# Attention with a gated block on one core: keys loaded in transposable order, weight sums stored in thirds, the key scale in the exponential, three raw weight chunks

## The chip, the cores and the metric

The kernel runs on one core of one Trainium2 chip. The metric is the device time of one execution in microseconds (us); lower is better.

## The reference, cut to what matters

```python
S, D, Hq, Dh, Sk, W, F = 2048, 640, 32, 192, 2048, 512, 1536      # all tensors bf16
xn = layernorm(x)                                                 # 2048 x 640, no gain or bias
q = (xn @ wq).reshape(S, 32, 192)                                 # wq: 640 x 6144
k, v = k_cache[:, Sk-W:], v_cache[:, Sk-W:]                       # last 512 positions of each head
p = softmax(einsum("qhd,hkd->hqk", q, k) * 192 ** -0.5)           # no mask
s = einsum("hqk,hkd->qhd", p, v).reshape(S, 6144) @ wo            # wo: 6144 x 640
h = sigmoid(xn @ w_gate) * (xn @ w_up)                            # gated block
out = x + s * silu(h @ w_down)
```

## The kernel before, in words

Two parts follow each other. The **gated block** works on four blocks of 512 rows (`s` = 0 to 3). For each of 12 slices `f` of the hidden width, PE multiplies by gate and up weights (L433), ACT takes the sigmoid (L438), and DVE multiplies both into `hT_sb` (L439). Then PE multiplies by `wd_sb` in four tiles of 128 rows (L485, 12 slices each, every one of which needs the whole of `hT_sb[:, f]`); ACT and DVE form the silu (L492, L493), and POOL stores the tile to DRAM (L499).

The **attention** works on pairs of heads, two pairs to a group, eight groups. A run is a group with one half of the rows (1024), so there are 16 runs, two for each group. Each run has 16 score groups (L625: six matmuls with the transposed keys `kT` into two PSUM banks, then the exponential on ACT, L629, from there into `E`), and then eight value products (L639), whose result DVE divides by the row sum (L645, L646) into `o_st`; SP transposes `o_st` by DMA (L652), and the product with `wo` of the run before (L682) is put between the value products. The queries of the next run are made between the score groups. `q_after` is the list written by hand that says which query slot follows which score group.

The queries are not made by a plain product. Rows and weights are cut in halves, and seven products of sums take the place of eight (`query_slots`): the weights stand in four forms for each group, `w0`, `TA`, `TB` and `TC`, each `[128, 5, 384]` in f16, of which partitions 0 to 63 and 64 to 127 hold different operands. Each matmul on them uses 64 partitions, and two run beside each other. The third `u` of a head's 192 columns is taken out of the weights with a step of three (`T[rr, c, u::PC]`, L576).

To get the weights into f16, the first part of the program finds the largest weight (`scan_load`, `scan_fold`, `set_scale`, `set_scale2`). All weights are multiplied by a power of two, `w_up` (L226), and the keys by its inverse, `w_down` (L150), so that the scores are right again. The weights of a group come in five chunks of 128 rows. For each chunk:

- `load_raw` (L211): two DMAs issued by POOL into one of two buffers `raw`.
- `scale_w` (L224): ACT scales the whole chunk in place (L226) and copies two parts into `w0` (L227, L228).
- `sum_w` (L230): DVE forms the sums `TB`, `TA`, `TC` (L233, L234, L236, L237), ACT copies one part (L235).

A buffer is loaded again only when the sums of the chunk before in it are done. `load_raw` stands in POOL's queue, so POOL waits there, and all that POOL issues afterwards waits too. For group 0 this goes on in the fourth block (`s` = 3), beside the sigmoids: `scale_w` after slices 0, 2, 5, 7, 10, `sum_w` after slices 1, 3, 6, 8, 11. For group 1 it is in run 0. For the later groups it is among the value products of the runs with the first half of the rows, by the lists `sum_at` and `scale_at`.

The keys of a pair of heads: `load_kn` (L138) loads one head as it lies in DRAM into one buffer `kn_sb` (POOL's queue); `sort_k` (L145) multiplies it on POOL by `w_down` and writes it into `k_sb` (one buffer) with the columns sorted by their remainder by three, in the order that the transpose takes; `turn_k` (L156) transposes `k_sb` by DMA on SP into one of two `kT`. Pair 0 of group g + 1 is turned at the start of the value products of the second run of group g, pair 1 after the fourth of these value products.

PSUM has eight banks; `bank2` gives them in pairs, 0 and 1 being pair 0. Score groups use banks 4 and 5 or 6 and 7 in turn. Everything else takes a pair from a ring, or from `bank_order` where this isn't empty. The first queries (run 0) have nothing to hide under; their results leave PSUM by ACT (`on_act`), and ACT's queue has the load of `wo_g` (L530) ahead of them.

Of the kernel before, what the change touches and what calls it, by code (L numbers as in the profile page):

```python
# [17 lines left out]
def kernel(  # L18
# [71 lines left out]
    ident = const.tile([P, P], BF16, name="ident")  # L90
    make_identity(nc, ident[:])

    eps_t = const.tile([P, 1], F32, name="eps_t")
    nc.vector.memset(eps_t[:], eps)

# [15 lines left out]
    raw_pool = qctx.enter_context(tc.tile_pool(name="raw_pool", bufs=2, **rs))  # L111
# [8 lines left out]
    mx = const.tile([P, 1], F32, name="mx")  # L120
    w_up = const.tile([P, 1], F32, name="w_up")
    w_down = const.tile([P, 1], F32, name="w_down")
# [13 lines left out]
    kn_of, k_of = {}, {}  # L136

    def load_kn(key, i=0):  # L138
        hk = (2 * (key[0] * G + key[1]) + i) // rep
        kn_of[key] = k_pool.tile([P, KC, DH], BF16, name="kn_sb")  # L140
        nc.gpsimd.dma_start(
            kn_of[key][:], A_k_cache[0, hk, Sk - W:Sk, :].rearrange("(p k) d -> p k d", k=KC),
        )

    def sort_k(key):  # L145
        k_sb = k_pool.tile([P, KC, PC, 2, HF], BF16, name="k_sb")
        for i in range(2):
            if i > 0:
                load_kn(key, i)
            nc.gpsimd.tensor_scalar(  # L150
                k_sb[:, :, :, i, :], kn_of[key][:].rearrange("p k (e j) -> p k j e", j=PC),
                w_down[:, 0:1], None, op0=ALU.mult,
            )
        k_of[key] = k_sb

    def turn_k(key):  # L156
        kT = kt_pool.tile([P, KC * PC, P], BF16, name="kT")
        nc.sync.dma_start_transpose(kT[:], k_of[key][:].rearrange("p k j i e -> p (k j i e)"))
        kT_t[key] = kT
# [37 lines left out]
    def set_scale(wm, mx_row):  # L197
        nc.vector.tensor_reduce(
            mx[:], wm[:].rearrange("p c n -> p (c n)"), axis=mybir.AxisListType.X, op=ALU.max)
        nc.gpsimd.dma_start(mx_d[:].rearrange("o p -> p o"), mx[:])  # L200
        nc.gpsimd.dma_start(mx_row[:], mx_d[:].to_broadcast([P, P]))

    def set_scale2(mx_row):
        nc.vector.tensor_reduce(mx[:], mx_row[:], axis=mybir.AxisListType.X, op=ALU.max)
        nc.vector.tensor_scalar(mx[:], mx[:], 1e-30, None, op0=ALU.max)
        bits = mx[:].bitcast(I32)
        nc.vector.tensor_single_scalar(bits, bits, 0x7F800000, op=ALU.bitwise_and)
        nc.vector.tensor_scalar(w_down[:], mx[:], 1.0 / 4096, None, op0=ALU.mult)
        nc.vector.reciprocal(w_up[:], w_down[:])
# [10 lines left out]
    def b(g, c, r, k, j):  # L220
        n = GC // 2
        return raw_t[g, c][r, k, j * n:(j + 1) * n].bitcast(F16)

    def scale_w(g, c):  # L224
        raw, w0 = raw_t[g, c][:], w_t[g][0]
        nc.scalar.activation(raw.bitcast(F16), raw, AF.Copy, scale=w_up[:, 0:1])  # L226
        nc.scalar.activation(w0[LO, c], b(g, c, LO, 0, 0), AF.Copy)  # L227
        nc.scalar.activation(w0[HI, c], b(g, c, HI, 1, 0), AF.Copy)  # L228

    def sum_w(g, c):  # L230
        _, TA, TB, TC = w_t[g]
        a, tt = slice(0, P), nc.vector.tensor_tensor
        tt(TB[:, c], b(g, c, a, 1, 1), b(g, c, a, 0, 1), ALU.subtract)  # L233
        tt(TA[:, c], TB[:, c], b(g, c, a, 0, 0), ALU.add)  # L234
        nc.scalar.activation(TB[HI, c], b(g, c, HI, 1, 1), AF.Copy)  # L235
        tt(TC[:, c], b(g, c, a, 1, 0), TA[:, c], ALU.subtract)  # L236
        tt(TA[HI, c], b(g, c, HI, 0, 1), b(g, c, HI, 0, 0), ALU.subtract)  # L237


    with ExitStack() as bctx:  # L240
# [7 lines left out]
        xt_pool = bctx.enter_context(tc.tile_pool(name="xt_pool", bufs=1))  # L248

# [171 lines left out]
        for s in range(NST):  # L421
# [4 lines left out]
            for f in range(NF):  # L426
# [30 lines left out]
                elif s == 2 and f < 4:  # L457
# [5 lines left out]
                elif s == 3:  # L463
# [36 lines left out]
            if s == 0:  # L500
                for hp in range(G):
                    load_v(0, hp, nc.gpsimd)
                for pp in range(1):
                    load_kn((0, pp))
# [9 lines left out]
    small = ctx.enter_context(tc.tile_pool(name="small", bufs=4))  # L514
# [32 lines left out]
    def query_slots(r, on_act, gamma):  # L547
# [27 lines left out]
        def wt(T, u):  # L575
            return lambda rr, c: T[rr, c, u::PC]  # L576
# [25 lines left out]
        def s4_split(u, bx, b):  # L602
# [4 lines left out]
        gx, gw, gy = gamma  # L607
        return [
            lambda: s1(0, 0, 1), lambda: s1(1, 2, 3),
            lambda: s2(0, 0, 1), lambda: s2(1, 2, 3),  # L610
            lambda: s3(0, 0, 1, False), lambda: s3(1, 2, 3, True),
            lambda: s4_pair(0, 0, 1, 1),
# [4 lines left out]
    def stage_s(r, i, pp, c, k):  # L617
# [11 lines left out]
        nc.scalar.activation(E_t[r, i, pp][:, c, :, :], ps, AF.Exp, scale=scale_qk)  # L629
# [92 lines left out]
    slots = query_slots(0, True, (4, 5, 6))  # L722
    for n, k in enumerate((0, 1, 7, 2, 3, 8, 4, 5, 9, 6, 10)):
# [112 lines left out]
```

## Time and profile before

| what | value |
|---|---|
| median of 3 runs | 952.66 us (951.15 to 952.68) |
| the profiled execution: time | 952.68 us |
| the profiled execution: span, first to last instruction | 950.9 us |
| mean granted clock of TensorE | 0.986 |
| DMA: packets, bytes | 186612, 100.37 MB |

How to read the lines: PE is TensorE's matmuls, PEld its weight loads, DVE VectorE, ACT ScalarE, POOL GpSimd, SP SyncE. A `q` behind an engine's name (SPq) is its queue, which issues DMAs. L226 is line 226 of the kernel. A group of instructions reads: line, engine, operation, written<-read by the names of the program, shapes, count | busy time in us, mean of one in ns | idle time of the engine just before them and what ended it. A line of the timeline reads: start in us, length in us, engine, line, operation, count, and in brackets the idle time before it with who ended that. A line of the waits reads: who waited <- for whom: us in total, times, the longest. A stretch reads: its two ends and length in us, then for each of PE, PEld, DVE, ACT, POOL that has instructions there the busy time and the count, then the granted clock, the share of the DMA engines, GB/s.

### The profile page before, as it was taken

What the parts mean: (1) busy time and instruction counts of PE and PEld (TensorE: products, weight loads), DVE (VectorE), ACT (ScalarE), POOL (GpSimd) and SP (SyncE); (2) the same over time, 40 slices, a digit from 0 to 9 for tenths busy, and PEclk for the clock granted to TensorE, in tenths of its full rate; (3) what the DMA queues carried; (4) which work ended last, traced back from release to release, by engine and by line L of the source; (5) the groups of instructions that cost most, each with busy time, mean ns of one, the idle gap of its engine ahead of it and who ended that gap; (6) DMA issues with size and microseconds to landing.
All of it is one profiled execution on the core that took longest, in us unless ns stands there. A gap on an engine that the chain in (4) does not pass through costs nothing. (4 is left out here: it accounts for less than half of the span.)

```text
span 950.9 us, 18447 instructions
## 1 busy us (share of the span) xinstructions
PE 904.0 (95%) x7706; PEld 552.2 (58%) x7785; DVE 652.6 (69%) x1090; ACT 446.0 (47%) x527; POOL 209.0 (22%) x216
## 2 busy tenths in 40 slices
PE   8999995689899999999999999999999999999987
PEld 5545442346475757575747575666566666666554
DVE  5879854357666776687668667866786678666556
ACT  4333362378425661566076607561755276423330
POOL 0042034110220132013202310321033002203951
PEclk9999999799899999999999999999999999999999
DMA  9875255222442456156415460635084416156724
GB/s 305 240 230 134 36 129 92 63 72 42 93 97 55 83 126 107 45 101 125 110 25 121 107 134 1 153 82 125 2 180 70 109 30 147 42 101 167 177 49 117
DMA packets 186612, 100.37 MB, mean 106 GB/s; under 512 B 153312, under 2 KB 178912, under 8 KB 186528
## 3 DMA queue, kind: packets, MB, share of 16 engines
q1 hardware_dynamic: 156848, 56.87, 28.8%
q0 software_dynamic: 9408, 29.93, 12.0%
q10 hardware_dynamic: 20272, 12.39, 5.0%
q8 instruction: 61, 1.00, 0.4%
q14 instruction: 23, 0.19, 0.1%
HBM read 57.87 MB, written 5.24 MB: 66 GB/s over the span
## 5 line engine op out<-in xcount | busy, mean ns | idle before, releaser
L629 ACT ACTIVATE E<-ps_all 128x1024 bf16<-128x1024 f32 x256 | 253.3, 1022 | 300.9 <-DMA v_sb<-in_A_v_cache_dram 165.2
L682 PE MATMUL ps_all<-wo_g,oT 128*128 128x128 bf16 (+2 forms) x1474 | 225.1, 296 | 6.4 <-DVE o_sb L697 3.1
L625 PE MATMUL ps_all<-qT,kT 64*128 64x512 bf16 x1536 | 199.4, 381 | 4.7 <-DVE o_st L646 3.0
L639 PE MATMUL ps_all<-v_sb,E 128*128 128x193 bf16 x2048 | 189.5, 247 | 2.4 <-DVE o_sb L697 1.8
L639 PEld LDWEIGHTS <-E 128*128 128x128 bf16 x2048 | 168.7, 98 | 20.9 <-issue 9.2
L682 PEld LDWEIGHTS <-oT 128*128 128x128 bf16 x1536 | 121.5, 98 | 82.5 <-issue 6.4
L573 DVE TENSOR_TENSOR qT<-ps_all,qp 128x512 bf16<-128x512 f32 x176 | 116.8, 688 | 53.0 <-PE ps_all L539 40.5
L560 DVE COPY qp<-ps_all 128x512 f32<-128x512 f32 x150 | 100.7, 688 | 61.5 <-PE ps_all L539 61.5
L214 POOL DMA_DIRECT2D raw<-in_A_wq_dram x80 | 47.9, 604 | 406.9 <-ACT wB L235 299.5
L625 PEld LDWEIGHTS <-kT 64*128 64x128 bf16 x1536 | 82.0, 95 | 89.6 <-issue 14.1
L646 DVE TENSOR_TENSOR o_st<-ps_all,rden 128x768 bf16<-128x768 f32 x128 | 122.5, 957 | 6.1 <-DMA oT<-o_st 1.7
L150 POOL TENSOR_SCALAR k_sb<-kn_sb,w_down 128x768 bf16<-128x768 bf16 x32 | 71.7, 2240 | 135.8 <-DMA kT<-k_sb 85.8
L226 ACT ACTIVATE raw<-raw,w_up 128x1536 f16<-128x1536 bf16 x40 | 63.0, 1575 | 43.0 <-DMA raw<-in_A_wq_dram 42.2
L485 PE MATMUL ps_all<-wd_sb,hT_sb 128*128 128x128 bf16 (+1 forms) x377 | 56.4, 310 | 15.7 <-DVE hT_sb L439 11.1
L439 DVE TENSOR_TENSOR hT_sb<-ps_all,sig_sb 128x512 bf16<-128x512 f32 x48 | 32.6, 684 | 41.0 <-ACT sig_sb L438 30.2
L539 PE MATMUL ps_all<-X,w 64*128 64x512 bf16 x420 | 52.7, 378 | 4.7 <-DVE o_st L646 2.9
L485 PEld LDWEIGHTS <-hT_sb 128*128 128x128 bf16 x384 | 30.9, 101 | 41.3 <-DVE hT_sb L439 11.7
L716 DVE TENSOR_TENSOR acc<-ps_all,acc 128x640 f32<-128x640 f32 x48 | 39.6, 825 | 21.9 <-PE ps_all L682 21.9
L539 PE MATMUL ps_all<-XA,wA 64*128 64x512 f16 x420 | 52.9, 376 | 1.3 <-ACT qp L558 0.9
L645 DVE RECIPROCAL rden<-ps_all 128x4 f32<-128x4 f32 x128 | 23.2, 181 | 44.5 <-PE ps_all L639 43.4
L539 PE MATMUL ps_all<-XB,wB 64*128 64x512 f16 x420 | 53.1, 376 | 0.4 <-ACT qp L558 0.2
L438 ACT ACTIVATE sig_sb<-ps_all 128x512 bf16<-128x512 f32 x48 | 28.1, 597 | 40.1 <-PE ps_all L433 37.1
(115 smaller groups left out, 766.8 us busy)
## 6 DMA issues: line engine op xcount, KB each, us to landing
raw<-in_A_wq_dram POOLq DMA_DIRECT2D x80, 192.0 KB, 4.2
wo_g<-in_A_wo_dram ACTq DMA_DIRECT2D x7, 960.0 KB, 5.2
kn_sb<-in_A_k_cache_dram POOLq DMA_DIRECT2D x32, 192.0 KB, 2.8
v_sb<-in_A_v_cache_dram ACTq DMA_DIRECT2D x28, 192.0 KB, 3.1
gB_d<-gB_sb POOLq DMA_DIRECT2D x16, 160.0 KB, 2.8
gBa_sb<-gB_d SPq DMA_DIRECT2D x16, 160.0 KB, 3.9
xa_sb<-in_A_x_dram SPq DMA_DIRECT2D x16, 160.0 KB, 3.8
out_dram<-o_sb SPq DMA_DIRECT2D x15, 160.0 KB, 1.8
```

The source lines that it names most:

```text
L150: nc.gpsimd.tensor_scalar(k_sb[:, :, :, i, :], kn_of[key][:].rearrange("p k (e j) -> p k j e", j=PC), w_down[:, 0:1], None, op0=ALU.mult,)
L214: eng.dma_start(raw[r], wq_r[:, c, :, g * GC:(g + 1) * GC])
L226: nc.scalar.activation(raw.bitcast(F16), raw, AF.Copy, scale=w_up[:, 0:1])
L485: nc.tensor.matmul(oB_ps[:, d0:d0 + dsz], lhsT=hT_sb[:, f, q * P:(q + 1) * P], rhs=wd_sb[:, f, d0:d0 + dsz], start=(f == 0), stop=(f == NF ...
L539: nc.tensor.matmul(ps_all[:, b, :], lhsT=w(r, c), rhs=x[r, c, :], start=(first and k == 0), stop=(k == len(cs) - 1), skip_group_check=True,)
L560: nc.vector.tensor_copy(dst, part(b))
L573: nc.vector.tensor_tensor(q_out(i, u, pp), part(b), t[:], ALU.add)
L625: nc.tensor.matmul(ps[:, b, :], lhsT=kT[h, c * PC + j, :], rhs=qT_t[r][i, j][h, pp, :], start=(j == 0), stop=(j == PC - 1),)
L629: nc.scalar.activation(E_t[r, i, pp][:, c, :, :], ps, AF.Exp, scale=scale_qk)
L639: nc.tensor.matmul(o_ps[:, q // 2, q % 2, 0:DH + 1], lhsT=E[:, c, h, q * P:(q + 1) * P], rhs=vt[:, c, 0:DH + 1], start=(c == 0), stop=(c = ...
L646: nc.vector.tensor_tensor(o_st[:, :, h * DH:(h + 1) * DH].rearrange("p (b i) d -> p b i d", b=2), o_ps[:, :, :, 0:DH], rden[:].to_broadcas ...
L682: nc.tensor.matmul(oA[:, d0 - base:d0 - base + dsz], lhsT=oT_t[r, i, pp][:, q * PC + j, :], rhs=wo_t[runs[r][1]][:, cc, d0:d0 + dsz], star ...
```

## The change

- **Keys.** `load_kn` and `sort_k` are gone. `load_k` loads both heads of a pair by two DMAs of POOL's queue straight into `k_sb`, 64 columns of a head at a time beside 64 of the other, which is the layout that `turn_k` takes. The columns are cut into three consecutive thirds instead of by the remainder by three.
- **Scale.** The keys are no longer multiplied. `w_down` is multiplied once by 192 ** -0.5 and is the exponential's scale, read from memory.
- **Weights.** The sums and `w0` are written in thirds, so that a query product takes 128 consecutive columns.
- **Raw chunks.** Three buffers; the third chunk of group 0 is loaded in the third block, each load is put three chunks ahead, and the lists are moved accordingly.
- **Order.** The first queries take banks 2 to 7 and 0 instead of 0 to 6; runs 0 and 15 begin their value products with pair 2.
- **Small tiles.** `ident` and `eps_t` go into a pool of the gated block; `mx`, `w_up` and `w_down` share a tile; `rden` has two buffers instead of four.

```diff
-    raw_pool = qctx.enter_context(tc.tile_pool(name="raw_pool", bufs=2, **rs))
+    raw_pool = qctx.enter_context(tc.tile_pool(name="raw_pool", bufs=3, **rs))
...
-    def load_kn(key, i=0):
-        hk = (2 * (key[0] * G + key[1]) + i) // rep
-        kn_of[key] = k_pool.tile([P, KC, DH], BF16, name="kn_sb")
-        nc.gpsimd.dma_start(
-            kn_of[key][:], A_k_cache[0, hk, Sk - W:Sk, :].rearrange("(p k) d -> p k d", k=KC),
-        )
-
-    def sort_k(key):
-        k_sb = k_pool.tile([P, KC, PC, 2, HF], BF16, name="k_sb")
+    def load_k(key):
+        k_sb = k_pool.tile([P, KC * PC, 2, HF], BF16, name="k_sb")
         for i in range(2):
-            if i > 0:
-                load_kn(key, i)
-            nc.gpsimd.tensor_scalar(
-                k_sb[:, :, :, i, :], kn_of[key][:].rearrange("p k (e j) -> p k j e", j=PC),
-                w_down[:, 0:1], None, op0=ALU.mult,
+            hk = (2 * (key[0] * G + key[1]) + i) // rep
+            nc.gpsimd.dma_start(
+                k_sb[:, :, i, :],
+                A_k_cache[0, hk, Sk - W:Sk, :].rearrange("(p k) (j e) -> p (k j) e", k=KC, e=HF),
             )
         k_of[key] = k_sb
...
         nc.vector.reciprocal(w_up, w_down)
+        nc.vector.tensor_scalar(w_down, w_down, scale_qk, None, op0=ALU.mult)
...
-    def b(g, c, r, k, j):
+    def part_w(g, c, r, k, j):
         n = GC // 2
-        return raw_t[g, c][r, k, j * n:(j + 1) * n].bitcast(F16)
+        w = raw_t[g, c][r, k, j * n:(j + 1) * n].bitcast(F16)
+        return w.rearrange("p (h j e) -> p h j e", h=2, e=HF)
+
+    def sums_w(g, c, r, i):
+        return w_t[g][i][r, c].rearrange("p (j h e) -> p h j e", h=2, e=HF)
...
-        tt(TB[:, c], b(g, c, a, 1, 1), b(g, c, a, 0, 1), ALU.subtract)
-        tt(TA[:, c], TB[:, c], b(g, c, a, 0, 0), ALU.add)
+        TA, TB, TC = (sums_w(g, c, a, i) for i in range(1, 4))
+        tt(TB, part_w(g, c, a, 1, 1), part_w(g, c, a, 0, 1), ALU.subtract)
+        tt(TA, TB, part_w(g, c, a, 0, 0), ALU.add)
...
-                elif s == 2 and f < 4:
+                elif s == 2 and f < 5:
                     load_raw(0, f - 2, nc.gpsimd)
...
                         sum_w(0, c)
-                        load_raw((c + 2) // NCD, (c + 2) % NCD, nc.gpsimd)
-                    if f == 2:
-                        sort_k((0, 0))
-                        turn_k((0, 0))
-                        load_kn((0, 1))
-                    elif f == 5:
-                        sort_k((0, 1))
-                        turn_k((0, 1))
-                        load_kn((1, 0))
+                        load_raw((c + 3) // NCD, (c + 3) % NCD, nc.gpsimd)
+                    if f in (2, 6):
+                        turn_k((0, f // 4))
+                        load_k(divmod(f // 4 + 1, G))
...
-            return lambda rr, c: T[rr, c, u::PC]
+            return lambda rr, c: T[rr, c, u * P:(u + 1) * P]
...
-        nc.scalar.activation(E_t[r, i, pp][:, c, :, :], ps, AF.Exp, scale=scale_qk)
+        nc.scalar.activation(E_t[r, i, pp][:, c, :, :], ps, AF.Exp, scale=w_down)
...
-    slots = query_slots(0, True, (4, 5, 6))
+    slots = query_slots(0, True, (2, 3), (4, 5), (6, 7, 0))
...
-            load_raw(1, n // 5 + 2, nc.gpsimd)
-    sum_at = {2: (3,), 4: (4,)}, {0: (0,), 1: (1,), 3: (2,), 5: (3,), 6: (4,)}
-    scale_at = {0: (3,), 2: (4,)}, {1: (2,), 3: (3,), 5: (4,)}
+            load_raw(1, n // 5 + 3, nc.gpsimd)
+    sum_at = {2: (3,), 6: (4,)}, {0: (0,), 1: (1,), 3: (2,), 4: (3,), 6: (4,)}
+    scale_at = {0: (3,), 2: (4,)}, {0: (2,), 3: (3,), 4: (4,)}
...
-            bank_order[:] = []
+            bank_order[:] = [2, 3, 0, 1] * 2
         else:
-            bank_order[:] = [0, 1, 0, 1] + [2, 3, 0, 1] * 3 if r > 0 else []
+            bank_order[:] = [0, 1, 0, 1] + [2, 3, 0, 1] * 3 if r > 0 else [2, 3, 0, 1] * 2
...
         elif pi == 1 and g + 1 < NG:
-            sort_k((g + 1, 0))
             turn_k((g + 1, 0))
-            load_kn((g + 1, 1))
-            sort_k((g + 1, 1))
-            if g + 2 < NG:
-                load_kn((g + 2, 0))
+            load_k((g + 1, 1))
...
             if k == 3 and pi == 1 and g + 1 < NG:
                 turn_k((g + 1, 1))
+                if g + 2 < NG:
+                    load_k((g + 2, 0))
...
-            for c in range(2):
+            for c in range(3):
                 load_raw(g + 2, c, nc.gpsimd)
```

More of the change, by code (lines that the diff above doesn't have):

```diff
@@ L119 @@
     w_t = {}
-    mx = const.tile([P, 1], F32, name="mx")
-    w_up = const.tile([P, 1], F32, name="w_up")
-    w_down = const.tile([P, 1], F32, name="w_down")
+    w_sc = const.tile([P, 3], F32, name="w_sc")
+    mx, w_up, w_down = (w_sc[:, i:i + 1] for i in range(3))
     NV = 2 * G
@@ L218, in weight_tiles @@
         w_t[g] = [wq_pool.tile([P, NCD, GC // 2], F16, name=f"w{i}") for i in "0ABC"]
-    def b(g, c, r, k, j):
+    def part_w(g, c, r, k, j):
         n = GC // 2
-        return raw_t[g, c][r, k, j * n:(j + 1) * n].bitcast(F16)
+        w = raw_t[g, c][r, k, j * n:(j + 1) * n].bitcast(F16)
+        return w.rearrange("p (h j e) -> p h j e", h=2, e=HF)
+    def sums_w(g, c, r, i):
+        return w_t[g][i][r, c].rearrange("p (j h e) -> p h j e", h=2, e=HF)
     def scale_w(g, c):
[L225 to L228, printed above, removed]
+        raw = raw_t[g, c][:]
+        nc.scalar.activation(raw.bitcast(F16), raw, AF.Copy, scale=w_up)
+        for k, r in enumerate((LO, HI)):
+            nc.scalar.activation(sums_w(g, c, r, 0), part_w(g, c, r, k, 0), AF.Copy)
     def sum_w(g, c):
-        _, TA, TB, TC = w_t[g]
         a, tt = slice(0, P), nc.vector.tensor_tensor
[L233 to L237, printed above, removed]
+        TA, TB, TC = (sums_w(g, c, a, i) for i in range(1, 4))
+        tt(TB, part_w(g, c, a, 1, 1), part_w(g, c, a, 0, 1), ALU.subtract)
+        tt(TA, TB, part_w(g, c, a, 0, 0), ALU.add)
+        nc.scalar.activation(sums_w(g, c, HI, 2), part_w(g, c, HI, 1, 1), AF.Copy)
+        tt(TC, part_w(g, c, a, 1, 0), TA, ALU.subtract)
+        tt(sums_w(g, c, HI, 1), part_w(g, c, HI, 0, 1), part_w(g, c, HI, 0, 0), ALU.subtract)
     with ExitStack() as bctx:
@@ L248 @@
         xt_pool = bctx.enter_context(tc.tile_pool(name="xt_pool", bufs=1))
+        ident = bone.tile([P, P], BF16, name="ident")
+        make_identity(nc, ident[:])
+        eps_t = bone.tile([P, 1], F32, name="eps_t")
+        nc.vector.memset(eps_t[:], eps)
         x_even = X1
@@ L789 @@
                     sum_w(new_t, c)
-                    if c + 2 < NCD:
-                        load_raw(new_t, c + 2, nc.gpsimd)
+                    if r > 0 and c + 3 < NCD:
+                        load_raw(new_t, c + 3, nc.gpsimd)
                 for c in scale_at[r > 0].get(k, ()):
```

41 lines of the change are left out of this document (18 added, 23 removed).

## The prediction

> **What bounds the kernel now.** I read the page first, then the stretches of the span, and then the timeline where a stretch shows idle time on the matrix engine.
>
> ```profile
> span 950.9 us, 18447 instructions
> PE 904.0 (95%) x7706; PEld 552.2 (58%) x7785; DVE 652.6 (69%) x1090; ACT 446.0 (47%) x527; POOL 209.0 (22%) x216
> ```
>
> PE is busy for 904.0 of 950.9 us, so 46.9 us idle are all that reordering can win, besides time lost to a slower clock. The change takes no matmul away. The stretches (us, then busy time of each engine, granted clock, DMA) say where the idle time lies:
>
> ```profile
> 151.80:185.90 34.10, 17.09 (x94) 8.62 (x96) 13.69 (x19) 11.36 (x16) 10.96 (x13) 0.80 0.35 73
> 203.60:228.10 24.50, 24.00 (x201) 11.74 (x200) 15.11 (x25) 18.96 (x21) 1.19 (x2) 0.93 0.11 30
> 242.00:248.00 6.00, 5.99 (x30) 2.56 (x31) 2.00 (x4) 2.05 (x2) 2.38 (x3) 0.51 0.96 218
> 291.00:890.00 599.00, 592.59 (x5473) 379.09 (x5523) 428.81 (x718) 304.18 (x341) 118.25 (x117) 1.00 0.44 93
> ```
>
> From 291 to 890 us, which is most of the sixteen attention runs, PE idles 599.00 - 592.59 = 6.4 us: little to win there. But in the 34.1 us in which the fourth gate block multiplies by wd_sb, 17.0 us are idle, and the clock that is granted afterwards is low (0.80 on average). The timeline of that stretch (start, length, engine, line, and in brackets the idle time before it and who ended it):
>
> ```profile
> 143.54 17.17 SPq L158 DMA_TRANSPOSE kT<-k_sb  x2
> 144.41 1.23 POOL L214 DMA_DIRECT2D raw<-in_A_wq_dram  x2
> 144.95 0.60 ACT L438 ACTIVATE sig_sb<-ps_all 128x512 bf16<-128x512 f32 x1
> 151.78 2.19 POOL L150 TENSOR_SCALAR k_sb<-kn_sb,w_down 128x768 bf16<-128x768 bf16 x1 [6.14 <-DMA kT<-k_sb]
> 152.51 1.57 ACT L226 ACTIVATE raw<-raw,w_up 128x1536 f16<-128x1536 bf16 x1 [6.97 <-DMA raw<-in_A_wq_dram]
> 155.85 4.62 PE L485 MATMUL ps_all<-wd_sb,hT_sb 128*128 128x512 bf16 x19 [4.06 <-ACT sig_sb L438]
> 167.94 1.57 ACT L226 ACTIVATE raw<-raw,w_up 128x1536 f16<-128x1536 bf16 x1 [9.10 <-DMA raw<-in_A_wq_dram]
> 172.00 6.23 PE L485 MATMUL ps_all<-wd_sb,hT_sb 128*128 128x512 bf16 x29 [9.99 <-DVE hT_sb L439]
> ```
>
> Read it backwards. PE waits for hT_sb, which needs the sigmoid on ACT. ACT works in order and stands in front of a weight chunk (L226) whose load has not landed. The load is late because POOL, which issues it, first sorts keys (L150) and waits for a key transpose to free k_sb. So two raw buffers and a sort on the loading queue cost this stage two stops.
>
> **The change, part by part.** *A, the fourth gate block.* Chunk 2 is now loaded in the block before. Chunk 3 goes out after the first sum, as chunk 2 did. Chunk 4 goes out after the second sum, and what stands ahead of it on POOL is only the two loads of key pair 1, not a sort. Those loads wait for the transpose of pair 0, which SP can issue as soon as its four swap copies are out, since its keys were loaded two blocks earlier. Both L226 waits (6.97 and 9.10 us) should go. What is late next is ACT itself. Durations:
>
> ```profile
> L226 ACT ACTIVATE raw<-raw,w_up 128x1536 f16<-128x1536 bf16 x40 | 63.0, 1575 | 43.0 <-DMA raw<-in_A_wq_dram 42.2
> L227 ACT ACTIVATE w<-raw 64x384 f16<-64x384 f16 x35 | 18.3, 523 | 1.1
> L235 ACT ACTIVATE wB<-raw 64x384 f16<-64x384 f16 x35 | 18.0, 513 | 25.4 <-DVE wA L234 25.4
> L439 DVE TENSOR_TENSOR hT_sb<-ps_all,sig_sb 128x512 bf16<-128x512 f32 x48 | 32.6, 684 | 41.0 <-ACT sig_sb L438 30.2 <-PE ps_all L433 10.5
> L234 DVE TENSOR_TENSOR wA<-wB,raw 128x384 f16<-128x384 f16 x35 | 12.5, 358 | 1.2
> ```
>
> The sigmoid of step 7 ends at 144.95 + 0.60 = 145.55. Scaling a chunk is 1.575 + 2 x 0.523 = 2.62, to 148.2; sigmoid 8 to 148.8; its hT 0.68, two sums 0.72 and L235's 0.51 bring ACT to 150.7; sigmoids 9 and 10 to 151.9; chunk 4 to 154.5; sigmoid 11 and its hT to 155.8. The down product starts at 155.85 - 4.06 = 151.8. Its length without waits is that of the block before (L485 alone):
>
> ```profile
> 92.00:125.70 33.70, 12.91 (x94) 7.42 (x96) 1.00 0.43 82
> ```
>
> 12.9 us for 48 steps, 0.27 each, so PE asks for hT 11 at 151.8 + 11 x 0.27 = 154.8: a wait of 1.0, 1.2 with hand-overs. The block ends at 151.8 + 12.9 + 1.2 = 165.9.
>
> ```profile
> 185.92 3.42 PE L539 MATMUL ps_all<-X,w 64*128 64x512 bf16 x30 [1.65 <-DVE gB_sb L493]
> 188.38 0.45 ACTq L530 DMA_DIRECT2D wo_g<-in_A_wo_dram  x1
> 203.63 0.61 PE L625 MATMUL ps_all<-qT,kT 64*128 64x512 bf16 x2 [1.22 <-DVE qT L573]
> ```
>
> Now it ends at 185.92 - 1.65 = 184.27. Gain **18.4**. The raw loads go out earlier still, so nothing waits behind them.
>
> *B, the first queries.* With products in banks 2 to 7 the first need not wait 1.65 us for the last gate tile. I cost that at nothing all the same: ACT is held until 188.38 by the load of wo_g, and ACT empties the banks, so the wait returns three products later. At the end, the first scores no longer share banks with the last query product: of 1.22 us what is left after one score group, about 0.5, comes back at the second (banks 6 and 7). Gain 0.7. The clock of 0.93 over 24.5 us is 1.7 us, which goes if the idle time shrinks; sum **2.4** (between 0 and 3.5).
>
> *C, between runs 0 and 1.* Run 0 has no output products, so its value products run faster than DVE empties them:
>
> ```profile
> 237.27 0.96 DVE L646 TENSOR_TENSOR o_st<-ps_all,rden 128x768 bf16<-128x768 f32 x1 [0.95 <-DMA oT<-o_st]
> 239.92 0.96 DVE L646 TENSOR_TENSOR o_st<-ps_all,rden 128x768 bf16<-128x768 f32 x1
> 242.01 2.74 PE L625 MATMUL ps_all<-qT,kT 64*128 64x512 bf16 x12 [3.04 <-DVE o_st L646]
> 242.08 0.96 DVE L646 TENSOR_TENSOR o_st<-ps_all,rden 128x768 bf16<-128x768 f32 x1
> ```
>
> Scores need banks 4 to 7, which now hold the last two value products. In the new order they hold the fifth and sixth. The fifth is empty at 237.27 + 0.96 = 238.2, before PE is done (242.01 - 3.04 = 238.97). The last weight sum moves behind the seventh, so the sixth follows after 1.1 (two take 242.08 - 239.92 = 2.16), at 239.3, and the seventh at 240.4, or some 0.9 later if its o_st waits for a transpose again. A score group takes 2.74 / 4 = 0.68 at the full clock, so two end at 240.3 and the first query slot waits up to 1.0; the second waits for the eighth, behind that weight sum, about as long. I put 0.85 and 0.95, so 3.04 becomes 1.8 (between 0 and 3.0). The half clock (0.51 over 6 us, 2.9 us lost) should go, since no wait is long. Gain **4.1** (1 to 6).
>
> *D, the other runs.* Waits from 291 to 890 us:
>
> ```profile
> DVE wB L233 <- ACT raw L226: 9.4, 6, 2.7
> PE ps_all L539 <- DVE o_st L646: 2.9, 4, 1.1
> ```
>
> DVE stands before sums whose chunk is not scaled, then empties the last value product late, and PE waits. With chunk 2 loaded a run ahead, and three steps between the loads of 3 and 4 and their use, the 9.4 should go. Gain **2.5** (-2 to 5; the lower end if the sums cost more, below).
>
> *E, the last run.*
>
> ```profile
> 920.42 10.83 PE L639 MATMUL ps_all<-v_sb,E 128*128 128x193 bf16 x128 [1.84 <-DVE o_sb L697]
> ```
>
> Its value products start in banks 4 and 5 instead of the banks that the last output product holds. Gain **1.8**.
>
> *What costs nothing.* Query weights are loaded contiguously instead of with a step of three:
>
> ```profile
> L539 PEld LDWEIGHTS <-wB 64*128 64x128 f16 x420 | 24.4, 100 | 22.3 <-issue 1.3
> L625 PEld LDWEIGHTS <-kT 64*128 64x128 bf16 x1536 | 82.0, 95 | 89.6 <-issue 14.1
> L629 ACT ACTIVATE E<-ps_all 128x1024 bf16<-128x1024 f32 x256 | 253.3, 1022 | 300.9 <-DMA v_sb<-in_A_v_cache_dram 165.2
> ```
>
> 100 ns becomes 95 under matmuls that are busy anyway. The exponential reads its scale from memory: by the slope from L227 to L226, (1575 - 523) / 1152 = 0.91 ns an element, 1024 elements take 1.11 us at most against 1.02; ACT's 300.9 us of idle time hide it. The 71.7 us of sorting leave POOL, which has no one waiting outside part A.
>
> The sum: 18.4 + 2.4 + 4.1 + 2.5 + 1.8 = 29.2. The profiled execution took 952.68 us (span 950.9 and 1.8 around it), equal to the median of 952.66: **923.5 us**.
>
> **The rivals.** *First: transposes still hold the last chunk.* The loads issued at 144.41, beside a transpose, gave ACT its chunk 8.1 us later. If chunk 4 goes out no earlier than 144.4, the second head's load waits for the first (4.4 us, a landing), and a transpose holds it as long, it is there at 144.4 + 4.4 + 8.1 = 156.9, 5 us after ACT asks for it at 151.9: 928.5. For it speaks that POOL must still wait for pair 0's transpose; against it, that this transpose no longer waits for a sort, as it did until 143.54.
>
> *Second: the sums slow down.* They now write runs of 64 elements.
>
> ```profile
> L195 DVE TENSOR_TENSOR wmax<-wmax,XB 128x1920 bf16<-128x1920 bf16 x3 | 3.5, 1157 | 0.1
> L195 DVE TENSOR_TENSOR wmax<-wmax,wA 128x1920 bf16<-128x1920 bf16 x2 | 2.3, 1159 | 0.1
> ```
>
> XB is read in five runs with gaps, wA in one piece, at the same price, which speaks against it; runs of 64 are not shown. At half the rate an operation gains (1157 - 358) / 1536 x 384 = 0.20 us; 20 in each of seven runs, none of it hidden: +28, so 951.5, no change.
>
> *Third, slower: the key loads come too late.* A head is now 1536 pieces of 128 bytes. One buffer is left, so in each of seven groups the load of pair 1 starts when the transpose of pair 0 has landed, and SP, in order, holds the output transposes behind that of pair 1.
>
> ```profile
> DMA to landing us min/median/max: 3.6/4.4/8.1
> 355.65 1.44 SPq L158 DMA_TRANSPOSE kT<-k_sb  x1
> 372.93 1.60 SPq L158 DMA_TRANSPOSE kT<-k_sb  x1
> q1 hardware_dynamic: 156848, 56.87, 28.8%
> L167 POOL DMA_DIRECT2D v_sb<-in_A_v_cache_dram x4 | 3.0, 756 | 0.0
> ```
>
> There are 372.93 - 355.65 - 4.4 = 12.9 us. Issuing 512 pieces takes 0.76 us, so a pair takes at most 6 x 0.76 = 4.5. SP's packets average 0.288 x 16 x 950.9 / 156848 = 28 ns for 363 bytes; 3072 / 16 x 28 ns = 5.4 us. Together 9.9: hidden. It decides from 17.4 us on, where 4.5 us too much, seven times, outweigh the gain; at 18 us the time is 959. The Trainium skill, DMA: Bandwidth & Descriptors, Specifications, says that pieces under 512 bytes are read, modified and written and miss the line rate; taken as twice the data time that is 10.8 + 4.5 = 15.3 us by my estimate, 2.4 us too much in seven groups, and a sum of 940 if nothing hid it. No run here shows such pieces from POOL's queue yet.
>
> **How the numbers follow.** The forecast has 0.80, the first rival 0.13, the second 0.05, the third 0.02. The range, 916 to 935, holds the forecast with its bounds (B, C and D at their good ends give some 7 less) and the first rival with B and D at their poor ends. About 0.2% (2 us) is what can be told from no change: faster 0.94; same 0.03, most of the second rival; slower 0.03, the rest of it and the third.
>
> **What would show it.** PE's stops in the fourth gate block sum to 1 to 3 us, and no L226 there waits for a load; the granted clock after it is 1.00; the stop before run 1 is under 2 us and the 0.51 is gone; value products of the last run start without a wait; PE's busy time falls only by what the clock gave back. I am wrong if L226 still waits over 3 us in that block, if the sums of 384 take over 0.4 us, or if kT is late in a later run.

## The result, and the profile after

The changed kernel takes 927.26 us, the median of four runs (923.96 to 927.78), against 952.67 (951.15 to 953.31) for the kernel before: a ratio of 0.9728, with a 95% interval of 0.9703 to 0.9754. That is 25.4 us faster, where 29.2 were forecast. The profiled execution took 927.78 us, 925.7 of it span. The page of the changed kernel:

```profile
span 925.7 us, 18472 instructions
PE 905.0 (98%) x7785; PEld 537.4 (58%) x7785; DVE 650.8 (70%) x1091; ACT 466.3 (50%) x527; POOL 151.1 (16%) x184
```

The two busy times (904.0 before, 905.0 now) cannot be set against each other as they stand. The profile of before has 7706 matmuls, this one 7785, with 7785 weight loads in both: 79 matmuls of before left no record, and their time counts as idle there. In the profile of before some 4 us of idle time ahead of the matmuls of L682, L485 and L433 have nothing that ended them, and there is nothing of the kind now. So of 46.9 us about 43 were idle, 925.7 - 905.0 = 20.7 are left, and of the 25.2 us by which the span is shorter about 22 are idle time and 3 the clock (both by my estimate). What is left has other reasons than before. These are PE's largest waits (total us, times, longest), without those of the output projection and the start:

```profile
PE ps_all L529 <- ACT qp L548: 2.5, 3, 2.0
PE ps_all L529 <- DVE o_st L636: 2.1, 1, 2.1
PE ps_all L529 <- DVE qT L563: 2.0, 2, 1.6
PE ps_all L615 <- ACT E L619: 1.7, 4, 1.0
PE ps_all L475 <- DVE hT_sb L434: 1.1, 1, 1.1
```

Lines have moved: the down product is L475 now, the query product L529, the scores L615, the value product L629, the exponential L619, the scaling of a raw chunk L216. To set the gain against the steps of the forecast I cut both spans at the same five places: the end of the fourth gate block (184.27 before; in the changed kernel the first query product follows at once), and the first value products of runs 0, 1, 14 and 15. Of before, from its timeline (the last of them, at 920.42, stands in the prediction):

```profile
228.13 10.84 PE L639 MATMUL ps_all<-v_sb,E 128*128 128x193 bf16 x128
266.79 1.42 PE L639 MATMUL ps_all<-v_sb,E 128*128 128x193 bf16 x15
866.11 1.51 PE L639 MATMUL ps_all<-v_sb,E 128*128 128x193 bf16 x16
```

Of after:

```profile
166.47 3.41 PE L529 MATMUL ps_all<-X,w 64*128 64x512 bf16 x30
209.56 10.83 PE L629 MATMUL ps_all<-v_sb,E 128*128 128x193 bf16 x128 [0.16 <-ACT E L619]
248.63 1.51 PE L629 MATMUL ps_all<-v_sb,E 128*128 128x193 bf16 x16
844.51 1.51 PE L629 MATMUL ps_all<-v_sb,E 128*128 128x193 bf16 x16
896.82 3.41 PE L629 MATMUL ps_all<-v_sb,E 128*128 128x193 bf16 x39
```

| stretch (us) | before | after | gain | forecast |
|---|---|---|---|---|
| A: start to the end of the fourth gate block | 184.27 | 166.47 | 17.8 | 18.4 |
| B: from there to run 0's value products | 43.86 | 43.09 | 0.8 | 2.4 |
| C: run 0's value products to run 1's | 38.66 | 39.07 | -0.4 | 4.1 |
| D: run 1's to run 14's | 599.32 | 595.88 | 3.4 | 2.5 |
| E: run 14's to run 15's | 54.31 | 52.31 | 2.0 | 1.8 |
| from there to the end of the span | 30.5 | 28.9 | 1.6 | 0 |
| around the span | 1.8 | 2.1 | -0.3 | 0 |
| sum | 952.7 | 927.8 | 24.9 | 29.2 |

So A, D and E came about as forecast or better, and what is missing lies in the 82 us of B and C. The fourth gate block of the changed kernel:

```profile
127.92 15.99 SPq L143 DMA_TRANSPOSE kT<-k_sb  x2
139.71 1.21 POOL L200 DMA_DIRECT2D raw<-in_A_wq_dram  x2 [0.51 <-ACT sig_sb L433]
156.32 9.90 PE L475 MATMUL ps_all<-wd_sb,hT_sb 128*128 128x512 bf16 x71 [1.10 <-DVE hT_sb L434]
```

The load of group 0's last chunk, chunk 4, in the kernel before (with the next group's first load behind it in the same row):

```profile
160.16 2.40 POOL L214 DMA_DIRECT2D raw<-in_A_wq_dram  x4
```

The first transpose goes out at 127.92 instead of 143.54, the load of chunk 4 at 139.71 instead of 160.16 (the load at 144.41 in the prediction is that of chunk 3), and of the stops of 4.06 and 9.99 us nothing is left but the 1.10 that the forecast put at 1.0 to 1.2. The page says of the scaling of chunks, over the whole kernel, that it hardly waits: its idle time was 43.0 us.

```profile
L216 ACT ACTIVATE raw<-raw,w_sc 128x1536 f16<-128x1536 bf16 x40 | 62.9, 1573 | 0.8
L619 ACT ACTIVATE E<-ps_all,w_sc 128x1024 bf16<-128x1024 f32 x256 | 275.3, 1114 | 280.0 <-PE ps_all L615 183.8
L135 POOL DMA_DIRECT2D k_sb<-in_A_k_cache_dram x32 | 32.9, 1029 | 264.1 <-DMA kT<-k_sb 207.6
```

The second row is a price: an exponential takes 1114 ns instead of 1022. Now the two places where PE stops. At the first queries:

```profile
170.80 0.44 ACTq L520 DMA_DIRECT2D wo_g<-in_A_wo_dram  x1
171.29 1.08 ACT L548 ACTIVATE qp<-ps_all 128x512 f32<-128x512 f32 x2 [4.00 <-DMA gB_d<-gB_sb]
171.94 0.37 PE L529 MATMUL ps_all<-XA,wA 64*128 64x512 f16 x1 [2.05 <-ACT qp L548]
```

ACT issues the load of wo_g, stands before it until the last gate rows are out, and only then empties the first bank (171.29), for which PE waits 2.05 us. Between runs 0 and 1:

```profile
222.90 0.96 DVE L636 TENSOR_TENSOR o_st<-ps_all,rden 128x768 bf16<-128x768 f32 x1 [1.96 <-DMA oT<-o_st]
223.91 1.30 PE L529 MATMUL ps_all<-X,acc_hi 64*128 64x512 bf16 x10 [2.12 <-DVE o_st L636]
224.55 0.52 ACT L225 ACTIVATE acc_hi<-raw 64x384 f16<-64x384 f16 x1 [5.70 <-DVE acc_hi L224]
225.09 2.12 ACT L619 ACTIVATE E<-ps_all,w_sc 128x1024 bf16<-128x1024 f32 x2
226.26 1.46 PE L615 MATMUL ps_all<-qT,kT 64*128 64x512 bf16 x6 [1.04 <-ACT E L619]
```

Two stops, 2.12 + 1.04 = 3.16 us. The seventh o_st stands 1.96 us before an output transpose that must free its tile, so the first query slot stands too. And the copy L225, which belongs to the weight sum that the change put behind the seventh product, stands on ACT, in order, ahead of the exponentials of run 1: 5.70 us idle, the first exponential only at 225.09, and the third score group waits 1.04 us for it.

After both stops the clock falls. The same profile cut into stretches as long as the clock keeps a value (busy times of PE, PEld, DVE, ACT, POOL, granted clock, DMA):

```profile
170.40:173.80 3.40, 1.46 (x12) 0.66 (x13) 1.29 (x2) 2.49 (x3) 0.00 (x0) 1.00 0.48 124
173.80:177.20 3.40, 3.40 (x19) 1.71 (x17) 1.42 (x4) 2.89 (x7) 0.00 (x0) 0.50 0.45 165
221.60:225.00 3.40, 1.28 (x12) 0.54 (x10) 2.00 (x5) 0.45 (x1) 0.00 (x0) 1.00 0.85 176
225.00:228.40 3.40, 2.36 (x14) 0.88 (x13) 2.72 (x5) 2.83 (x4) 1.19 (x2) 0.50 0.36 80
228.40:231.80 3.40, 3.40 (x20) 1.38 (x18) 1.38 (x2) 1.10 (x2) 0.00 (x0) 0.50 0.81 152
```

Three stretches of 3.41 us at half clock, each behind one in which PE was busy for less than half, or which itself was at half clock. The four runs fit that: 923.96 us at a mean clock of 1.000, and 927.78, 927.30 and 927.22 at 0.993 to 0.994.

### The profile page after: what moved, and what is told of

The parts are those of the page before. It is cut to its first block, busy times and chain, and to the rows that moved or that the text cites. A ratio compares the mean times of both kernels' runs of the same rounds, so it can differ in the third digit from the quotient of the medians.

```text
span 925.7 us, 18472 instructions
## 1 busy us (share of the span) xinstructions
PE 905.0 (98%) x7785; PEld 537.4 (58%) x7785; DVE 650.8 (70%) x1091; ACT 466.3 (50%) x527; POOL 151.1 (16%) x184
## 5 line engine op out<-in xcount | busy, mean ns | idle before, releaser
L619 ACT ACTIVATE E<-ps_all,w_sc 128x1024 bf16<-128x1024 f32 x256 | 275.3, 1114 | 280.0 <-PE ps_all L615 183.8
L672 PE MATMUL ps_all<-wo_g,oT 128*128 128x512 bf16 (+2 forms) x1536 | 228.4, 299 | 3.1 <-DVE o_sb L687 3.1
L615 PE MATMUL ps_all<-qT,kT 64*128 64x512 bf16 x1536 | 199.4, 378 | 2.3 <-ACT E L619 1.7
L629 PE MATMUL ps_all<-v_sb,E 128*128 128x193 bf16 x2048 | 189.5, 247 | 0.2 <-ACT E L619 0.2
L629 PEld LDWEIGHTS <-E 128*128 128x128 bf16 x2048 | 168.7, 98 | 18.2 <-issue 6.4
L615 PEld LDWEIGHTS <-kT 64*128 64x128 bf16 x1536 | 77.2, 94 | 93.4 <-issue 14.3
L135 POOL DMA_DIRECT2D k_sb<-in_A_k_cache_dram x32 | 32.9, 1029 | 264.1 <-DMA kT<-k_sb 207.6
L216 ACT ACTIVATE raw<-raw,w_sc 128x1536 f16<-128x1536 bf16 x40 | 62.9, 1573 | 0.8
L529 PE MATMUL ps_all<-XA,wA 64*128 64x512 f16 x420 | 54.1, 385 | 2.5 <-ACT qp L548 2.0
L475 PE MATMUL ps_all<-wd_sb,hT_sb 128*128 128x512 bf16 (+1 forms) x384 | 53.1, 299 | 1.1 <-DVE hT_sb L434 1.1
L529 PE MATMUL ps_all<-XB,wB 64*128 64x512 f16 x420 | 52.8, 376 | 0.5 <-ACT qp L548 0.5
L529 PE MATMUL ps_all<-X,w 64*128 64x512 bf16 x420 | 51.9, 376 | 0.0
L433 ACT ACTIVATE sig_sb<-ps_all 128x512 bf16<-128x512 f32 x48 | 28.1, 596 | 40.2 <-PE ps_all L428 37.1
L706 DVE TENSOR_TENSOR acc_hi<-ps_all,acc_hi 128x640 f32<-128x640 f32 x48 | 39.3, 818 | 7.8 <-PE ps_all L672 7.8
```

The source lines that it names most:

```text
L475: nc.tensor.matmul(oB_ps[:, d0:d0 + dsz], lhsT=hT_sb[:, f, q * P:(q + 1) * P], rhs=wd_sb[:, f, d0:d0 + dsz], start=(f == 0), stop=(f == NF ...
L529: nc.tensor.matmul(ps_all[:, b, :], lhsT=w(r, c), rhs=x[r, c, :], start=(first and k == 0), stop=(k == len(cs) - 1), skip_group_check=True,)
L615: nc.tensor.matmul(ps[:, b, :], lhsT=kT[h, c * PC + j, :], rhs=qT_t[r][i, j][h, pp, :], start=(j == 0), stop=(j == PC - 1),)
L629: nc.tensor.matmul(o_ps[:, q // 2, q % 2, 0:DH + 1], lhsT=E[:, c, h, q * P:(q + 1) * P], rhs=vt[:, c, 0:DH + 1], start=(c == 0), stop=(c = ...
L672: nc.tensor.matmul(oA[:, d0 - base:d0 - base + dsz], lhsT=oT_t[r, i, pp][:, q * PC + j, :], rhs=wo_t[runs[r][1]][:, cc, d0:d0 + dsz], star ...
L706: nc.vector.tensor_tensor(acc[t][:], oA[:, 0:D], acc[t][:], ALU.add)
```

## The experiments

**Which part cures the fourth gate block.** My theory was that both were needed: keys off POOL's queue, and a third raw buffer. Keys alone, with two raw buffers and the lists and banks of before (against the changed kernel; the lists go back in the same way):

```diff
-    raw_pool = qctx.enter_context(tc.tile_pool(name="raw_pool", bufs=3, **rs))
+    raw_pool = qctx.enter_context(tc.tile_pool(name="raw_pool", bufs=2, **rs))
...
-                elif s == 2 and f < 5:
+                elif s == 2 and f < 4:
...
-                        load_raw((c + 3) // NCD, (c + 3) % NCD, nc.gpsimd)
+                        load_raw((c + 2) // NCD, (c + 2) % NCD, nc.gpsimd)
...
-            bank_order[:] = [2, 3, 0, 1] * 2
+            bank_order[:] = []
...
```

> The kernel before with the key part alone (keys loaded straight in transposable order, scale in the exponential, weights in thirds); two raw buffers, the lists and banks of before. My theory now: the two stops in the fourth gate block came from POOL's queue, where the loads of chunks 3 and 4 stood behind the sort; without the sort two buffers are enough there, so the stops fall from 15.2 us to under 4 us and the whole is about 936 us (952.7 less 18 in that block, plus about 2 for the slower exponential; the waits from 291 us on stay). Rival: the third buffer does it; then chunk waits of 5 us and more stay in that block and the whole is 943 us or more.

936.89 us (935.20 to 937.34), ratio 0.9823 (0.9807 to 0.9838), as the theory had it. Five of PE's waits in it:

```profile
PE ps_all L529 <- DVE o_st L636: 4.6, 6, 1.1
PE ps_all L615 <- DVE o_st L636: 3.3, 1, 3.3
PE ps_all L629 <- DVE o_sb L687: 1.8, 1, 1.8
PE ps_all L529 <- DVE gB_sb L483: 1.7, 1, 1.7
PE ps_all L475 <- DVE hT_sb L434: 1.3, 2, 1.1
```

The down product waits 1.3 us instead of 15.2 (11.1 and 4.1 in the waits of before): keys alone cure the block. Of the rest of the changed kernel's gain little is there: runs 1 to 14 take 602.48 us, longer than before (599.32), because the waits for o_st stay and the exponentials are slow; the 1.7 and the 1.8 stay as well.

The reverse puts a pass over the keys back onto POOL, ahead of each transpose, and keeps three buffers (multiplied by 1.0, so the keys stay what they are):

```diff
+    def pass_k(key):
+        for i in range(2):
+            nc.gpsimd.tensor_scalar(k_of[key][:, :, i, :], k_of[key][:, :, i, :], 1.0, None, op0=ALU.mult)
...
-                    if f in (2, 6):
+                    if f in (2, 5):
+                        pass_k((0, f // 4))
                         turn_k((0, f // 4))
...
```

> The changed kernel (927.3 us) with work on POOL put back in front of each key transpose: two multiplications of the keys by 1.0 in place, as long as the sort was, the first two after slices 2 and 5 of the fourth block. Three raw buffers stay. Theory (POOL's queue is the cause): chunk 4 of group 0 goes out only after the pass and the transpose of pair 0, and the fourth block has stops of 3 to 10 us again: 930 to 938 us. Rival (the third buffer is what counts): chunk 4 is still early enough, stops under 2 us, 927 to 929 us.

926.79 us (925.69 to 927.16), ratio 0.9721 (0.9705 to 0.9737). My theory fell and the rival held: there are two short stops in the block, 1.84 us together.

```profile
155.28 0.45 PE L480 MATMUL ps_all<-wd_sb,hT_sb 128*128 128x512 bf16 x2 [0.73 <-DVE hT_sb L438]
156.83 10.23 PE L480 MATMUL ps_all<-wd_sb,hT_sb 128*128 128x512 bf16 x73 [1.11 <-DVE hT_sb L438]
```

The pass did hold POOL up: chunk 4's load goes out at 147.21 instead of 139.71. But with three buffers ACT still has the chunk in time, since its 40 scalings stand idle for 0.8 us in all. So keys alone are enough, and with a third buffer work on POOL ahead of the transposes does no harm. That the third buffer alone is enough is not shown: this kernel keeps the new way of loading the keys, and the raw part without the key part was not run.

**Whether the slow exponential is hidden.** The scale is given as a number in the instruction, the value that w_down has for these weights:

```diff
-        nc.scalar.activation(E_t[r, i, pp][:, c, :, :], ps, AF.Exp, scale=w_down)
+        nc.scalar.activation(E_t[r, i, pp][:, c, :, :], ps, AF.Exp, scale=scale_qk * 2.0 ** -19)
```

> The changed kernel with the exponential's scale as a constant of the instruction (the value that w_down has for these weights) instead of read from memory. Theory: the exponential falls from 1.11 to 1.02 us, each of the middle runs' score stretches from 22.02 back to 21.90 us, and the whole by about 2 us, to 925.3 us. Rival (the exponential is hidden, as I had said): the instruction is shorter and the time stays at 927.3 us.

923.91 us (921.88 to 926.60), ratio 0.9691 (0.9666 to 0.9717). The page's row, and the first value products of runs 1 and 2:

```profile
L619 ACT ACTIVATE E<-ps_all 128x1024 bf16<-128x1024 f32 x256 | 253.2, 1022 | 298.6 <-PE ps_all L615 227.7 <-DMA v_sb<-in_A_v_cache_dram 70.8
```

```profile
249.02 1.51 PE L629 MATMUL ps_all<-v_sb,E 128*128 128x193 bf16 x16
294.74 1.51 PE L629 MATMUL ps_all<-v_sb,E 128*128 128x193 bf16 x16
```

A run takes 294.74 - 249.02 = 45.72 us, against 294.47 - 248.63 = 45.84 in the changed kernel. All thirteen stretches between runs 1 and 14 are that long, within 0.01 us, in either kernel, so 13 x 0.12 = 1.6 us are shown. They arise in a run's last score groups, where PE gets to the last query slot 0.13 us later after a score group than with the constant; in the profile that is too short to be listed as a wait. The rest of the difference of the medians lies within the spread of the runs.

**The stop at the first queries.** The load of wo_g goes behind the query slots:

```diff
-    load_wo(0)
     slots = query_slots(0, True, (2, 3), (4, 5), (6, 7, 0))
...
+    load_wo(0)
     sum_at = {2: (3,), 6: (4,)}, {0: (0,), 1: (1,), 3: (2,), 4: (3,), 6: (4,)}
```

> The changed kernel with the load of the first wo_g moved behind the first queries in ACT's order. Theory: ACT was held by that load until the last gate tile was in DRAM; without it the wait of 2.05 us in the first queries goes, and with it the half clock that follows (3.4 us at half rate, 1.7 us): 923.5 to 925.5 us. Rival: the first copies out of PSUM write memory that the gate tiles held and wait for the same store; then nothing changes, 927.3 us.

923.91 us (923.61 to 926.71), ratio 0.9696 (0.9677 to 0.9715). The wait of 2.05 for ACT is gone, and PE runs on to the next one:

```profile
174.22 3.40 PE L529 MATMUL ps_all<-XA,wA 64*128 64x512 f16 x29 [1.27 <-DVE qT L563]
```

That is the theory. In this profile the stretch B, from 169.33 to 209.71, takes 40.38 us instead of 43.09 and has no half clock: of these 2.7 us about 1.2 are shorter stops and the rest the clock. The medians alone would not show it, as the runs of the two kernels overlap. The half clock came elsewhere in this execution: the fourth block had two stops of 0.93 and 1.11 us close together, and the 3.4 us from 157.89 ran at half clock.

**The stop between runs 0 and 1.** Run 0's last weight sum goes back to its place of before:

```diff
-    sum_at = {2: (3,), 6: (4,)}, {0: (0,), 1: (1,), 3: (2,), 4: (3,), 6: (4,)}
+    sum_at = {2: (3,), 4: (4,)}, {0: (0,), 1: (1,), 3: (2,), 4: (3,), 6: (4,)}
```

> The changed kernel with the last weight sum of run 0 back behind the fifth value product (before: fifth, changed: seventh). In the changed kernel PE stands 2.12 us before run 1's first query slot and 1.04 us before its third score group. Theory: the 1.04 us come from ACT, where the copy of that late sum (L225) stands ahead of run 1's exponentials, and the 2.12 us from the seventh value product, whose o_st waits for a transpose; with the sum earlier the 1.04 us go and the 2.1 us stay: about 1 us less than 927.3. Rival: the sum earlier delays the sixth and seventh value products on DVE, the stop grows to 3 us or more, and the time is 927.3 us or above.

923.18 us (922.84 to 926.75), ratio 0.9703 (0.9679 to 0.9727).

```profile
221.71 0.52 ACT L225 ACTIVATE acc_hi<-raw 64x384 f16<-64x384 f16 x1 [1.35 <-DVE acc_hi L224]
222.70 1.11 ACT L619 ACTIVATE E<-ps_all,w_sc 128x1024 bf16<-128x1024 f32 x1 [0.47 <-PE ps_all L615]
223.72 0.82 PE L615 MATMUL ps_all<-qT,kT 64*128 64x512 bf16 x6 [1.07 <-DVE o_st L636]
225.41 1.26 PE L529 MATMUL ps_all<-X,acc_hi 64*128 64x512 bf16 x10 [0.86 <-DVE o_st L636]
```

L225 is out of the way at once, the exponentials start at 222.70, and no score group waits for one: the 1.04 us go, as the theory said. What I had not expected is that the other stop shrinks too: 1.07 + 0.86 = 1.93 us for o_st instead of 2.12. The clock stays at 1.00 there, and the stretch between the value products takes 35.06 us instead of 39.07: 3.16 - 1.93 = 1.2 from the stops, the other 2.8 from the clock. So to put that sum later, as the change did, was a loss: of 1.2 us in the stops, and in this profile of the clock as well.

The same sum put into run 1, behind its first query slot:

```diff
-    sum_at = {2: (3,), 6: (4,)}, {0: (0,), 1: (1,), 3: (2,), 4: (3,), 6: (4,)}
+    sum_at = {2: (3,)}, {0: (0,), 1: (1,), 3: (2,), 4: (3,), 6: (4,)}
...
+            elif r == 1 and k == 1:
+                sum_w(1, 4)
+                load_raw(2, 2, nc.gpsimd)
...
```

> The changed kernel with the last weight sum of group 1 taken out of run 0's value products and put behind the first query slot of run 1 (the load that needs its buffer goes with it). Theory as in the run with the sum behind the fifth product: nothing stands ahead of the exponentials any more, the stop of 1.04 us goes, that of 2.1 us stays, 926.0 to 926.5 us, 2 us less still if the half clock of 6.8 us after it shortens to one stretch of 3.4. Rival (DVE's total work between the runs sets the stop): both stops shrink.

925.74 us (923.01 to 926.38), ratio 0.9715 (0.9693 to 0.9737): stops of 1.88 and 0.45 us, and 35.45 us between the value products. No better than the place of before.

**What contiguous weights are worth.** Everything as in the changed kernel, but PE loads each query weight with a step of three, so that columns are paired otherwise than in the reference:

```diff
-            return lambda rr, c: T[rr, c, u * P:(u + 1) * P]
+            return lambda rr, c: T[rr, c, u::PC]
```

> The changed kernel with PE reading the weights with a step of three again, as before the change (the columns that it multiplies are therefore not those of the keys: this leaves the right pairing of columns out and shows only the price of the reading). Theory: weight loads of the query products take 100 ns instead of 94 and hide under the matmuls; 927.3 us, within 1.5. Rival: contiguous loads are part of the gain; then the middle runs take more than 45.84 us each and the whole is 929 us or more.

924.69 us (924.17 to 929.90), ratio 0.9720 (0.9690 to 0.9751): no difference that can be told, as forecast, and a middle run takes 45.83 us as against 45.84, though a load takes 100 ns with the step and 94 to 98 without. The profile of this kernel gave more than that. It has the changed kernel's stops (2.04 us at 171.81, 2.04 and 1.08 at 223.07 and 225.41), but its clock is 1.00 all through:

```profile
167.70:171.10 3.40, 2.06 (x20) 0.88 (x17) 0.31 (x1) 0.00 (x0) 0.54 (x1) 1.00 0.13 48
171.10:174.50 3.40, 2.28 (x19) 1.24 (x20) 1.29 (x2) 3.27 (x5) 0.00 (x0) 1.00 0.76 222
218.90:222.30 3.40, 2.13 (x20) 1.05 (x19) 1.55 (x5) 0.00 (x0) 0.00 (x0) 1.00 1.20 203
222.30:225.70 3.40, 1.55 (x14) 0.78 (x15) 3.23 (x8) 1.97 (x3) 0.70 (x2) 1.00 0.33 61
```

In this execution the borders of the stretches fall into the stops (171.1, 222.3), so that each stop is shared by two of them. In the last row PE is busy for 1.55 us and the clock stays, where 1.46 was too little in the changed kernel. Without the half clock, run 0's value products are 36.34 us ahead of run 1's: the same instructions as in the changed kernel but for the step of the weights, 2.7 us less. The stretch B takes 42.37 us at full clock, only 0.7 less than the 43.09 with 3.4 us at half clock, in part because PE waits 0.69 us for ACT at 175.60, where the slower PE had not.

**Three edits together.** The load of wo_g as above; the last sum of group 1 and the chunk loads of group 2 in run 1; and run 1's first seven query slots one score group later each:

```diff
...
+    q_one = {2: (0,), 3: (1,), 4: (2,), 5: (3,), 6: (4,), 7: (5, 6), 8: (7,), 10: (8,), 12: (9,), 14: (10,)}
...
-            for j in q_after.get(k, ()) if q_list else ():
+            for j in (q_one if r == 1 else q_after).get(k, ()) if q_list else ():
...
+            elif r == 1 and k == 1:
+                sum_w(1, 4)
+                for c in range(3):
+                    load_raw(2, c, nc.gpsimd)
...
```

> The changed kernel with three edits: wo_g's first load behind the first queries, the last weight sum of group 1 and the loads of group 2's first chunks in run 1, and run 1's first seven query slots each one score group later. Theory: of the stops between runs 0 and 1 (3.2 us) about 1 us is left and the clock stays up there, and the first queries lose 1.6 us of idle time: 920 to 923 us. Rival: the clock falls all the same, since the stops only move: 924 us or more.

921.76 us (920.63 to 923.93), ratio 0.9683 (0.9660 to 0.9707), the fastest of all: each of its five runs is at or below 923.93, each of the changed kernel's four at or above 923.96. Its stops between runs 0 and 1:

```profile
219.16 0.82 PE L615 MATMUL ps_all<-qT,kT 64*128 64x512 bf16 x6 [0.56 <-ACT E L619]
220.41 1.26 PE L529 MATMUL ps_all<-X,acc_hi 64*128 64x512 bf16 x10 [0.43 <-DVE o_st L636]
223.85 0.82 PE L615 MATMUL ps_all<-qT,kT 64*128 64x512 bf16 x6 [0.45 <-ACT E L619]
```

1.44 us in three pieces instead of 3.16 in two, and a mean clock of 0.999 in the profiled execution. It still has the slow exponential.

## Why the prediction was right and where it was wrong

*A was right in mechanism and size* (17.8 us for 18.4). The block starts 0.3 us later than before, and the 12.9 us for the down product were 0.3 short: two of the 96 matmuls are missing in that row, and from first to last the block before took 13.20. One point of its reasoning was too strict: it blamed two raw buffers and the sort together, and with the keys out of POOL's way two buffers are enough.

*E was right*, 2.0 for 1.8: the 1.84 us are gone.

*B: the mechanism was right, the clock was not.* The wait for the last gate tile did come back behind ACT and the load of wo_g (2.05 us), and 0.57 for the expected 0.5 came back at the second score group. The failed step is "1.7 us, which goes if the idle time shrinks": 2.05 us of idle time were enough for another 3.4 us at half clock. The 1.7 was also the most that it could bring: without a half clock B was shorter by 0.7 us with strided weights, and by some 1.5, the stops aside, with the later wo_g. 0.8 instead of 2.4.

*C was wrong, and it is most of the miss.* Two steps failed. "The last weight sum moves behind the seventh, so ... 3.04 becomes 1.8": I followed that sum on DVE alone. It has an instruction on ACT as well, which now stands ahead of the exponentials, and moved the stop to them (1.04 us); with the sum in its old place the stops are 1.93 us, near the 1.8, and 3.16 with the move. And the wait of the seventh o_st for its transpose, which I put at "some 0.9", was 1.96. The second step was "the half clock should go, since no wait is long": a 2.12-us wait brought it back, for 6.8 us. With the clock at 1.00 the stretch would have taken 36.34 us, a gain of 2.3, within my bounds of 1 to 6.

*D came out near the forecast by two errors that partly cancel.* There was more to win than the 2.5 that I put. Before, six of the thirteen stretches between runs 1 and 14 took 45.82 to 47.56 us and the other seven 45.72: 5.0 us too much in all, of which the trace lists 3.7 as PE's waits for o_st. All thirteen have the same length now, so no wait for o_st is left. But "ACT's 300.9 us of idle time hide it" was false: the exponentials are in the chain of a run's last score groups, and 0.12 us per run came through, 1.6 in all. Idle time over the whole span says nothing on the few exponentials for which PE waits. Without that price D would have gained 5.0; that 3.4 is near 2.5 is luck.

*The end.* 1.6 us behind the last run's first value product were not forecast: from the last DVE instruction to the end of the span it is 2.92 us now and was 4.59. All eight experiments have 2.9 to 3.2, the one with the key part alone too. There is one profile of before, and no run tells why; it stays open, so 1.6 of the 24.9 us have no cause shown.

*The rivals.* Transposes did not hold the last chunk. The sums did not slow down:

```profile
L224 DVE TENSOR_TENSOR wA<-wB,raw 128x384 f16<-128x384 f16 x35 | 12.5, 358 | 1.2
L226 DVE TENSOR_TENSOR wC<-raw,wA 128x384 f16<-128x384 f16 x35 | 12.5, 358 | 1.2
```

358 ns in runs of 64, where the same two took 358 and 392 before. The key loads are slower, but not late. Issuing a head takes 1029 ns (the L135 row above), and landing:

```profile
k_sb<-in_A_k_cache_dram POOLq DMA_DIRECT2D x32, 192.0 KB, 4.6
```

That is 2 x 1.03 + 4.6 = 6.7 us for a pair at the median, and 8.6 with the slowest landing (6.5), of the 12.9 that there are; PE never waits for kT. The Trainium skill (DMA: Bandwidth & Descriptors, Specifications) says that pieces under 512 bytes miss the line rate. A head landed after 2.8 us before and after 4.6 now, which agrees in direction; these loads are hidden, so no run here prices that rule in time of the kernel.

## What to carry to other kernels

When a step is moved, follow each of its instructions on its own engine: the DVE part of this weight sum went where it did no harm, its one copy on ACT went ahead of run 1's exponentials. Idle time summed over the span does not hide a slower instruction; look at the one stretch where another engine waits for it. And where a stop is about 2 us long, its price is its length plus half a clock for 3.4 or 6.8 us with some chance, so it should pay to break one long stop into short ones even if their sum stays; no run here kept the sum and changed only that.

## What the hardware showed that I had not expected

**The clock falls after stops shorter than 3.4 us, and the phase decides.** In every profile the clock changes at multiples of 3.413 us from its first change, the end of the span aside. I cut the profiles of both kernels and the eight experiments into such windows and summed PE's idle time in each, without the gaps of missing matmul records. Of windows at full clock, 51 with 0.7 to 1.62 us idle were all followed by full clock, 22 with 1.94 to 3.41 us idle were all followed by half clock (three more end with their span), and of eight between (1.65 to 1.87) two were. So in these traces about half a window of idle time decides, and as the windows lie differently in each execution (the first border is between 4.3 and 7.2 us in these ten), a stop of 2 us falls into one window or is shared by two. That would explain why the same kernel gave 923.96 and 927.78: only the slower of these two executions left a trace, but that of the kernel with strided weights shows the same stops at full clock. The Trainium skill (TensorE: Matmul & The Clock Gate, What's actually happening) has the free-running window of 3413 ns, and the traces agree with it; it asks for an idle window of some 3.4 us for half clock, and here the measurement differs: 1.94 us in one window sufficed.

**A scale from memory costs an activation 92 ns** (1114 against 1022 ns for 128 x 1024, with nothing else changed). The Trainium skill (ScalarE: Activation LUTs, What ACT_TABLE_LOAD costs) gives about 93 ns for each such operand, and the trace agrees. My slope gave the same 1.11 us, but by luck: it runs from L227, which reads no scale from memory, to L226, which does, and so spread that fixed price over the elements. What I missed was where it counts.
